# Where the next block's planes are cast and subtracted at the seams of a split-precision MLP

## The chip, the core and the metric

The kernel runs on one core of a Trainium2 chip. The core has five engines, each with its own queue of instructions that it works off in order: TensorE (PE, matmuls; its weight loads are shown as PEld), VectorE (DVE), ScalarE (ACT), GpSimd (POOL) and SyncE (SP, which here only issues DMAs). Engines wait for each other on semaphores. The metric is the device time of one execution in microseconds; the figure for the kernel before is the median of three runs.

## The reference

A transformer block with adaptive layer norm on one sequence of S = 2048 rows of D = 448, all float32: six modulation rows from `c`, attention with 16 heads, then an MLP with F = 1792.

```python
x = A_x
mod = (_silu(c) @ w_mod).reshape(c.shape[0], 6, 1, -1)
sa, ca, ga, sb, cb, gb = (mod[:, 0], mod[:, 1], mod[:, 2], mod[:, 3], mod[:, 4], mod[:, 5])
h = _layernorm(x, axis=-1) * (1 + ca) + sa
x = x + ga * _A_ref(h, A_wqkv, A_wo)
h = _layernorm(x, axis=-1) * (1 + cb) + sb
x = x + gb * _B_ref(h, B_w1, B_b1, B_w2, B_b2)

def _B_ref(x, w1, b1, w2, b2):
    y = _layernorm(x, axis=-1)
    h = _gelu(jnp.einsum("bsd,df->bsf", y, w1) + b1)
    return jnp.einsum("bsf,fd->bsd", h, w2) + b2
```

The change lies in `_B_ref`, the MLP, alone.

## The kernel before, in words

**Stages.** The kernel first makes the modulation rows, q, k and v, then runs attention (most of the span), and ends with the MLP, which takes the stretch from about 820 us on. The instructions are issued in an order written out by hand: each engine's queue holds its instructions in the order in which the Python code emits them.

**Split precision.** A float32 operand of a matmul is cut into two planes of the matmul's type: "hi", a rounded copy, and "lo", what is left when hi is subtracted. A product is then hi·hi + hi·lo + lo·hi, so making an operand ready costs one cast and one subtraction, and the subtraction needs the cast.

**The MLP.** The rows are worked in NB = 4 blocks b of 512 rows, the hidden features in NFT = 14 tiles i of 128. For every (b, i), `mlp1` (L1418) runs a W1 chain of eleven matmuls (L396), applies the gelu on ScalarE (L1428), casts its result (L1431, on ScalarE for block 0 and on VectorE for the others) and subtracts on VectorE (L1432). `mlp2` (L1456) multiplies the two planes of a gelu by W2, twelve matmuls of lines 1472 to 1474, and after the fourteenth tile adds and stores the block (L1478, L1479). The loop at L1482 issues `mlp1` of step n and `mlp2` of step n - LAG, LAG = 2, so a gelu has about two chains and two W2 blocks of time until TensorE wants it. The W1 chains take their accumulators in turn from a ring of three.

**The order inside a W1 chain** is that of `terms448` (L400): for each of the planes k = 0, 1, 2 of the block's rows, hi times both planes of W1 (six matmuls), then the three lo planes (three), then plane 3, which holds both its hi rows and its lo rows (two).

**The next block's rows.** `ln2_stages` (L1105 onwards) gives two functions for each block. `stage(i)` holds the second layer norms, spread over the steps of the block before; for blocks 1 to 3 it ends with a transpose on VectorE, a store to a scratch tensor in DRAM (`send`, L1142) and a load of four chunks in turned order (`fetch`, L1152). For block 1 the fetch is issued at step i = 11 of block 0, for blocks 2 and 3 at step i = 9 of the block before. `chunk(k)` (L1177), for k = 0 to 3, makes the planes: the cast `act.copy` on ScalarE (L1192) and the subtraction on VectorE (L1193). Block 0 takes the transposes on TensorE in place of the fetch; it isn't reached by the change.

**Room for the planes.** A block has seven plane tiles: hi of k = 0 to 2, lo of k = 0 to 2, and the shared one of k = 3. They take their places from eight tags in a ring (L1180), so plane n of a block takes the place that plane n - 1 of the block before had, and plane 0 takes the spare one.

**A seam** is the step of (b, 13) with b = 0, 1 or 2, the last of a block. Before the change it issues, in this order: the W1 chain of (b, 13), its gelu, cast and subtraction; W1 and W2 tiles that are still to be prepared (`w_prep.step()`, L1490, only in block 0: at its last step a product with the row gb on VectorE at L1240, a cast on ScalarE at L1242 and a subtraction on VectorE at L1243); chunks 0 and 1 of the next block; `mlp2(b, 11)`; chunks 2 and 3. Then follow the chain of (b + 1, 0) and `mlp2(b, 12)`.

```python
yT[b] = (lambda k: tiles[k] if k < 3 else tiles[6], lambda k: tiles[3 + k])
...
act.copy(hi, p)
dve.tensor_tensor(out=lo[rs_], in0=p[rs_], in1=f(hi)[rs_], op=ALU.subtract)
```

Of the kernel before, what the change touches and what calls it, by code (L numbers as in the profile page):

```python
# [26 lines left out]
NC = 4  # L27
NB = S // 512
NG = H // 4
NKT = S // 128  # L30
NFT = F // 128
# [13 lines left out]
def tile_adaln_block(ctx: ExitStack, tc: tile.TileContext, x, wqkv, wo, w1, b1, w2, b2, c, w_mod, out):  # L45
# [29 lines left out]
    def nm(t):  # L75
        uid[0] += 1
        return f"{t}_{uid[0]}"

    def sbt(tag, shape, dt=F32, bufs=1):
        return sb.tile(shape, dt, tag=tag, name=nm(tag), bufs=bufs)  # L80
# [27 lines left out]
    def ps_mx():  # L108
        mx_ring.append(mx_ring.pop(0))
        return ps_tile(mx_ring[-1], 1 if mx_ring[-1] == "m1" else 2)  # L110
# [7 lines left out]
    def f(t):  # L118
        return t.bitcast(F32)
# [272 lines left out]
    def mm_acc(p, terms, mid=None):  # L392
        for i, (a, b) in enumerate(terms):
            if mid and i == len(terms) // 2:
                mid()
            pe.matmul(p, a, b, start=(i == 0), stop=(i == len(terms) - 1))  # L396
# [3 lines left out]
    def terms448(x_hi, x_lo, w_hi, w_lo):  # L400
        ts = []
        for k in range(3):
            ts += [(x_hi(k), w_hi(k)), (x_hi(k), w_lo(k))]
        ts += [(x_lo(k), w_hi(k)) for k in range(3)]
        ts += [(x_hi(3), w_lo(3)), (x_hi(3), w_hi(3))]
        return ts
# [411 lines left out]
    for b in range(NB):  # L818
# [12 lines left out]
        for n, (tb, kind, g) in enumerate(tasks):  # L831
# [9 lines left out]
            k = n - (6, 4, 4, 4)[b]  # L841
# [19 lines left out]
            if more:  # L861
                k = n - (6, 4, 4, 4)[b]
# [417 lines left out]
    lnst = [ln2_stages(b) for b in range(NB)]  # L1280
# [134 lines left out]

    ov = out[0].rearrange("(b p t) n -> b p t n", p=128, t=4)

    def mlp1(b, i):  # L1418
        q, ii = divmod(i, 4)
        w_hi, w_lo = w1t[q]  # L1420
        fs = slice(ii * 128, (ii + 1) * 128)
        p = ps_mx()
        ts = terms448(*yT[b], lambda k: w_hi(k)[:, fs], lambda k: w_lo(k)[:, fs])
        mm_acc(p, [(w, y) for y, w in ts])
        gf = sbt("full", [128, 512], bufs=3)
        if (b, i) == (0, 0):
            act.activation(gf[:, 0:1], zero_col, AF.Gelu_apprx_tanh)
        act.activation(gf, p, AF.Gelu_apprx_tanh, bias=b1_col[:, i : i + 1])  # L1428
        ghi = sbt("hi", [128, 512], F32R, bufs=3)
        glo = sbt("lo", [128, 512], F32R, bufs=3)  # L1430
        (dve.tensor_copy if b else act.copy)(ghi, gf)  # L1431
        dve.tensor_tensor(out=glo, in0=gf, in1=f(ghi), op=ALU.subtract)  # L1432
        gs[(b, i)] = (ghi, glo)

    load_o(NB - 2, 2, "c1")
    load_o(NB - 2, 3, "c0h")
    mlp1(0, 0)
    av(*pend)
    end_unit(pend[0], pend[3])
# [16 lines left out]
    def mlp2(b, m):  # L1456

        if m == 0 and b < NB - 1:
            om[b] = [s2[:, j] for s2 in (ps_s2(), ps_s2()) for j in range(2)]
        elif m == 0:  # L1460
            for key in ("s1", "s0"):
                ps_close(key)
            for t in range(4):
                ps_open(f"t{t}")
            om[b] = [ps_tile(f"t{t}") for t in range(4)]
        ghi, glo = gs.pop((b, m))
        q, ii = divmod(m, 4)
        w_hi, w_lo = w2t[q][0](ii), w2t[q][1](ii)
        for t in range(4):
            ts = slice(t * 128, (t + 1) * 128)  # L1470
            pp = om[b][t][:, :D]
            pe.matmul(pp, ghi[:, ts], w_hi, start=(m == 0), stop=False)  # L1472
            pe.matmul(pp, ghi[:, ts], w_lo, start=False, stop=False)  # L1473
            pe.matmul(pp, glo[:, ts], w_hi, start=False, stop=(m == NFT - 1))  # L1474
        if m == NFT - 1:
            for t in range(4):
                ot = xn_t()
                dve.tensor_tensor(out=ot[:, :D], in0=om[b][t][:, :D], in1=acc[b][:, t, :], op=ALU.add)  # L1478
                sp.dma_start(ov[b][:, t, :], ot[:, :D])  # L1479

    seq = [(b, i) for b in range(NB) for i in range(NFT)]
    for n in range(len(seq) + LAG):  # L1482
        if n < len(seq):
            b, i = seq[n]
            if n:
                mlp1(b, i)
            for fn in tail.pop(n, ()):
                fn()
            for _ in range(2 if n % 2 else 1):
                w_prep.step()  # L1490
            if b + 1 < NB:
                lnst[b + 1][0](i)
            if b:
                lnst[b][0](20 + i)
        ahead = n < len(seq) and i == NFT - 1 and b + 1 < NB
        if ahead:
            for k in range(2):
                lnst[b + 1][1](k)
        if n >= LAG:
            mlp2(*seq[n - LAG])  # L1500
        if ahead:
            for k in range(2, NC):
                lnst[b + 1][1](k)
    for key in ("t3", "t2", "t1", "t0", "m2", "m1", "o"):
        ps_close(key)

# [34 lines left out]
```

## Time and profile before

| | |
|---|---|
| median of three runs | 1099.84 us (1099.55 to 1100.01) |
| the profiled execution's own time | 1099.75 us |
| its span in the profile | 1097.5 us |
| granted TensorE clock | 1.00 |
| W1 chain, eleven matmuls | 2.56 us |
| a gelu on ScalarE (L1428) | 0.69 us |
| a cast of a plane (L1192), alone | 0.62 us |
| a subtraction of a plane (L1193), alone | 0.68 us |

How to read it: the profile is of one execution, times are from the start of its span, and the time of a run is 2.25 us longer than the span. In a timeline row stand the start, the duration, the engine, the line of the kernel, the operation, what it writes and reads, the count of instructions that were merged, and in brackets the idle time ahead of it on its engine with what ended it. Consecutive instructions of one engine overlap a little, so a merged row of four is shorter than four single ones. In a list of waits a row names who waited, for whom, the sum in us, the number of times and the longest.

### The profile page before, as it was taken

What the parts mean: (1) busy time and instruction counts of PE and PEld (TensorE: products, weight loads), DVE (VectorE), ACT (ScalarE), POOL (GpSimd) and SP (SyncE); (2) the same over time, 40 slices, a digit from 0 to 9 for tenths busy, and PEclk for the clock granted to TensorE, in tenths of its full rate; (3) what the DMA queues carried; (4) which work ended last, traced back from release to release, by engine and by line L of the source; (5) the groups of instructions that cost most, each with busy time, mean ns of one, the idle gap of its engine ahead of it and who ended that gap; (6) DMA issues with size and microseconds to landing.
All of it is one profiled execution on the core that took longest, in us unless ns stands there. A gap on an engine that the chain in (4) does not pass through costs nothing.

```text
span 1097.5 us, 20709 instructions
## 1 busy us (share of the span) xinstructions
PE 1088.1 (99%) x8255; PEld 658.3 (60%) x8255; DVE 805.1 (73%) x1382; ACT 697.6 (64%) x883; POOL 198.7 (18%) x201
## 2 busy tenths in 40 slices
PE   8999999999999999999999999999999999999998
PEld 6756675444444444444444444554488788888887
DVE  6968788999999999988888888575655565463322
ACT  4565667888888888888888888678933411211211
POOL 1543332210000000000000000217123042061000
PEclk9999999999999999999999999999999999999999
DMA  9563354121222201232211213111442302002000
GB/s 312 207 190 103 97 188 134 59 65 32 72 76 64 77 28 41 67 98 54 69 48 38 86 49 104 58 31 59 136 137 65 101 34 55 18 34 72 34 1 34
DMA packets 58438, 88.57 MB, mean 81 GB/s; under 512 B 13759, under 2 KB 25686, under 8 KB 58330
## 3 DMA queue, kind: packets, MB, share of 16 engines
q1 hardware_dynamic: 57858, 86.51, 26.3%
q8 instruction: 65, 1.06, 0.4%
q10 hardware_dynamic: 148, 0.46, 0.1%
q0 software_dynamic: 336, 0.28, 0.1%
q14 instruction: 31, 0.25, 0.1%
HBM read 59.39 MB, written 29.50 MB: 81 GB/s over the span
## 4 chain that ended last, share of the span: by engine, by line
PE 96%; DVE 2%; DMA 1%; ACT 1%; issue 0%; SPq 0%; DVEq 0%; ACTq 0%
PE s L1382 23%; PE o L1337 23%; PE m L396 16%; PE pa L396 9%; PE m L476 8%; PE s L1472 3%; PE s L1473 3%; PE s L1474 3%; PE s L476 2%; PE t L1473 1%; PE t L1474 1%; PE t L1472 1%; DVE y L1193 1%; DMA slot_c<-in_w_mod_dram 1%; PE o L277 1%; DVE mxp L481 0%
## 5 line engine op out<-in xcount | busy, mean ns | idle before, releaser
L481 DVE TENSOR_REDUCE mxp<-m 128x1 f32<-128x512 f32 x555 | 359.7, 685 | 65.0 <-PE m L476 49.6
L1382 PE MATMUL s<-slot_b,slot_a 28*128 28x512 f32 (+1 forms) x3072 | 356.7, 423 | 0.0
L1382 PEld LDWEIGHTS s<-slot_b,slot_a 28*128 28x128 f32 (+1 forms) x3072 | 211.1, 183 | 176.0 <-ACT slot_c L1395 96.4
L476 PE MATMUL m<-kh,qh 28*128 28x512 f32 x607 | 226.9, 468 | 0.5 <-DVE mxp L481 0.3
L1395 ACT ACTIVATE slot_c<-s 128x1024 f32<-128x1024 f32 x170 | 174.7, 1028 | 51.6 <-PE s L1382 50.8
L1337 PE MATMUL o<-slot_c,v 128*32 128x512 f32 x680 | 178.9, 605 | 0.0
L1428 ACT ACTIVATE full<-m,b_col 128x512 f32<-128x512 f32 x56 | 38.6, 689 | 206.6 <-PE m L396 201.4
L686 DVE TENSOR_REDUCE mxp<-s 128x2 f32<-128x1024 f32 x107 | 131.1, 1226 | 5.1
L1337 PE MATMUL o<-slot_c1h,v 128*32 128x512 f32 x512 | 134.7, 605 | 0.0
L1337 PE MATMUL o<-slot_c0h,v 128*32 128x512 f32 x508 | 133.6, 605 | 0.0
L1395 ACT ACTIVATE slot_c1h<-s 128x1024 f32<-128x1024 f32 x128 | 130.7, 1021 | 0.0
L1395 ACT ACTIVATE slot_c0h<-s 128x1024 f32<-128x1024 f32 x127 | 130.5, 1028 | 0.0
L1395 ACT ACTIVATE slot_d<-s 128x1024 f32<-128x1024 f32 x86 | 88.4, 1028 | 25.0 <-PE s L1382 24.7
L1431 DVE CAST hi<-full 128x512 fp32r<-128x512 f32 x42 | 18.7, 444 | 112.3 <-ACT full L1428 112.3
L476 PEld LDWEIGHTS m<-kh,qh 28*128 28x128 f32 x607 | 90.7, 182 | 15.2 <-DVE mxp L481 13.1
L1337 PE MATMUL o<-slot_d,v 128*32 128x512 f32 x344 | 90.5, 605 | 0.4 <-ACT osb L1301 0.4
L1062 POOL TENSOR_TENSOR osb<-osb,osb 128x512 f32<-128x512 f32 x16 | 20.6, 1286 | 362.8 <-DMA osb<-drec 343.5
L1432 DVE TENSOR_TENSOR lo<-full,hi 128x512 fp32r<-128x512 f32 x56 | 46.0, 822 | 29.7 <-ACT hi L1431 25.1
L396 PE MATMUL m<-y,slot_a 128*128 128x512 f32 x160 | 60.9, 397 | 0.4 <-DVE y L1193 0.2
L481 DVE TENSOR_REDUCE mxp<-ma 128x1 f32<-128x512 f32 x61 | 39.5, 681 | 13.2 <-PE m L476 9.2
L1337 PEld LDWEIGHTS o<-slot_c,v 128*32 128x32 f32 x680 | 24.5, 108 | 39.1 <-issue 36.5
L650 DVE CUSTOM_DVE_ANT_0 slot_d0i<-m,slot_d0i 128x512 f32<-128x512 f32 x54 | 37.3, 691 | 14.3 <-PE m L476 11.3
(351 smaller groups left out, 1824.2 us busy)
## 6 DMA issues: line engine op xcount, KB each, us to landing
slot_b<-d SPq DMA_DIRECT2D x32, 256.0 KB
slot_a<-d SPq DMA_DIRECT2D x32, 256.0 KB
d<-lo SPq DMA_DIRECT2D x28, 256.0 KB
d<-hi SPq DMA_DIRECT2D x16, 256.0 KB
osb<-drec SPq DMA_DIRECT2D x15, 256.0 KB
out_dram<-xn SPq DMA_DIRECT2D x16, 224.0 KB
raw<-in_B_w_dram SPq DMA_DIRECT2D x14, 224.0 KB
qh<-d SPq DMA_DIRECT2D x12, 256.0 KB
```

The source lines that it names most:

```text
L396: pe.matmul(p, a, b, start=(i == 0), stop=(i == len(terms) - 1))
L476: pe.matmul(m, qh_sb[(g, qt)][js, i * 128 : (i + 1) * 128], k[js, :], start=True, stop=True)
L481: dve.tensor_reduce(out=mxp[(g, qt)][:, i, j, cch : cch + 1], in_=m, op=ALU.max, axis=AX.X)
L686: dve.tensor_reduce(out=mxp[(g, qt)][:, i, j : j + 2, cch], in_=t, op=ALU.max, axis=AX.X)
L1337: pe.matmul(o[32 * j : 32 * j + 32, :], v_sb[kt // 4][:, kt % 4, 4 * g + j, :], p[j // 2][:, j % 2, :], start=(kt == 0), stop=(kt == NKT - 1),
L1382: pe.matmul(s2[:, jj, :], ks[rows_, kp, kc], qs[rows_, qp, :], start=(term == 0), stop=(term == 2))
L1395: act.activation(pt[hf], s2, AF.Exp, scale=SCALE)
L1428: act.activation(gf, p, AF.Gelu_apprx_tanh, bias=b1_col[:, i : i + 1])
L1432: dve.tensor_tensor(out=glo, in0=gf, in1=f(ghi), op=ALU.subtract)
L1472: pe.matmul(pp, ghi[:, ts], w_hi, start=(m == 0), stop=False)
L1473: pe.matmul(pp, ghi[:, ts], w_lo, start=False, stop=False)
L1474: pe.matmul(pp, glo[:, ts], w_hi, start=False, stop=(m == NFT - 1))
```

## The change

The four calls of `chunk` for the next block move from behind the step's other work into `mlp1`, between the last matmul of the chain of (b, 13) and the gelu that reads it. `mlp1` gets an argument `mid`, a function that is called there; `seam(b)` gives one that calls the four chunks of block b. It is passed at i = 13 of blocks 0, 1 and 2 only.

```diff
-    def mlp1(b, i):
+    def mlp1(b, i, mid=None):
         q, ii = divmod(i, 4)
...
         mm_acc(p, [(w, y) for y, w in ts])
+        if mid:
+            mid()
         gf = sbt("full", [128, 512], bufs=3)
...
+    def seam(b):
+        return lambda: [lnst[b][1](k) for k in range(NC)]
+
     seq = [(b, i) for b in range(NB) for i in range(NFT)]
     for n in range(len(seq) + LAG):
         if n < len(seq):
             b, i = seq[n]
             if n:
-                mlp1(b, i)
+                mlp1(b, i, seam(b + 1) if i == NFT - 1 and b + 1 < NB else None)
...
-        ahead = n < len(seq) and i == NFT - 1 and b + 1 < NB
-        if ahead:
-            for k in range(2):
-                lnst[b + 1][1](k)
         if n >= LAG:
             mlp2(*seq[n - LAG])
-        if ahead:
-            for k in range(2, NC):
-                lnst[b + 1][1](k)
```

## The prediction

> **What bounds the kernel now.** I read the page's head first, then the list of waits from 820 us on (the MLP's stretch), then the timeline around each of the three places where one block of 512 rows gives way to the next.
>
> ```profile
> span 1097.5 us, 20709 instructions
> PE 1088.1 (99%) x8255; PEld 658.3 (60%) x8255; DVE 805.1 (73%) x1382; ACT 697.6 (64%) x883; POOL 198.7 (18%) x201
> ```
>
> TensorE is busy 1088.1 of 1097.5 us, so an edit that removes no matmul can win only what TensorE stands idle. Who makes it wait in the MLP:
>
> ```profile
> PE m L396 <- ACT y L1192: 1.4, 1, 1.4
> PE m L396 <- DVE y L1193: 0.2, 1, 0.2
> PEld m L396 <- ACT y L1192: 2.2, 3, 1.7
> PEld m L396 <- DVE y L1193: 1.6, 3, 0.5
> ```
>
> All four rows are W1 matmuls (line 396) that wait for the next block's planes: L1192 is the cast, L1193 the subtraction. The PE and PEld rows show the same idle time twice, so the rows are not added up; the timeline gives the sum. First seam (block 0 to 1), TensorE:
>
> ```profile
> 875.21 0.37 PE L1474 MATMUL s<-slot_d0i,lo 128*128 128x448 f32 x1
> 876.94 0.50 PE L396 MATMUL m<-y,slot_b 128*128 128x512 f32 x1 [1.36 <-ACT y L1192]
> 879.60 0.50 PE L396 MATMUL m<-y,slot_a 128*128 128x512 f32 x1 [0.19 <-DVE y L1193]
> 880.17 0.37 PE L1472 MATMUL s<-slot_e,hi 128*128 128x448 f32 x1
> 882.38 0.36 PE L1474 MATMUL s<-slot_e,lo 128*128 128x448 f32 x1
> 885.13 0.37 PE L1472 MATMUL s<-slot_e,hi 128*128 128x448 f32 x1
> ```
>
> From the last W2 matmul ahead of a W1 chain to the first one behind it are 885.13 - 882.38 = 2.75 us where nothing is late (second chain of block 1) and 880.17 - 875.21 = 4.96 us at the seam. **Lost: 2.21 us.** Seams two and three:
>
> ```profile
> 947.59 0.37 PE L1474 MATMUL s<-slot_d0i,lo 128*128 128x448 f32 x1
> 950.13 0.19 PEld L396 LDWEIGHTS m<-y,slot_a 128*128 128x128 f32 x1 [0.52 <-DVE y L1193]
> 950.70 0.37 PE L1472 MATMUL s<-slot_e,hi 128*128 128x448 f32 x1
> 952.97 0.37 PE L1474 MATMUL s<-slot_e,lo 128*128 128x448 f32 x1
> 955.73 0.37 PE L1472 MATMUL s<-slot_e,hi 128*128 128x448 f32 x1
> 1018.21 0.37 PE L1474 MATMUL s<-slot_d0i,lo 128*128 128x448 f32 x1
> 1020.74 0.19 PEld L396 LDWEIGHTS m<-y,slot_a 128*128 128x128 f32 x1 [0.51 <-DVE y L1193]
> 1021.32 0.37 PE L1472 MATMUL s<-slot_e,hi 128*128 128x448 f32 x1
> ```
>
> Here the interval is 3.11 us twice, against 955.73 - 952.97 = 2.76: **0.35 us each**, and only the last subtraction is late. All three seams lose 2.21 + 0.35 + 0.35 = 2.91 us. The bound on any gain is therefore about 2.9 us.
>
> Why the planes are late at the first seam, on ScalarE and then VectorE:
>
> ```profile
> 870.85 0.57 ACT L1242 CAST slot_e<-full 128x448 fp32r<-128x448 f32 x1 [1.34 <-DVE full L1240]
> 873.17 0.69 ACT L1428 ACTIVATE full<-m,b_col 128x512 f32<-128x512 f32 x1 [1.75 <-PE m L396]
> 873.89 0.62 ACT L1431 CAST hi<-full 128x512 fp32r<-128x512 f32 x1
> 875.80 0.56 ACT L1242 CAST slot_e<-full 128x448 fp32r<-128x448 f32 x1 [1.29 <-DVE full L1240]
> 876.27 2.18 ACT L1192 CAST y<-xn 128x512 fp32r<-128x512 f32 x4
> ...
> 874.54 0.69 DVE L1432 TENSOR_TENSOR lo<-full,hi 128x512 fp32r<-128x512 f32 x1 [2.47 <-ACT hi L1431]
> 875.15 0.62 DVE L1240 TENSOR_TENSOR full<-raw,row_gb 128x448 f32<-128x448 f32 x1
> 876.40 0.63 DVE L1243 TENSOR_TENSOR slot_e<-full,slot_e 128x448 fp32r<-128x448 f32 x1 [0.63 <-ACT slot_e L1242]
> 876.94 2.61 DVE L1193 TENSOR_TENSOR y<-xn,y 128x512 fp32r<-128x512 f32 x4
> ```
>
> The four casts stand on ScalarE behind a ladder: gelu, its copy, VectorE's subtraction, VectorE's product with the row gb, then the cast of the last W2 tile at 875.80. That cast is the releaser, not the data: ScalarE goes straight from it to the plane casts. At seams two and three there is no W2 tile; the casts come right behind the gelu, and the subtractions behind the gelu's own cast and subtraction:
>
> ```profile
> 945.60 0.69 ACT L1428 ACTIVATE full<-m,b_col 128x512 f32<-128x512 f32 x1 [4.32 <-PE m L396]
> 946.19 2.17 ACT L1192 CAST y<-xn 128x512 fp32r<-128x512 f32 x4
> ...
> 946.86 0.69 DVE L1432 TENSOR_TENSOR lo<-full,hi 128x512 fp32r<-128x512 f32 x1
> 947.47 2.61 DVE L1193 TENSOR_TENSOR y<-xn,y 128x512 fp32r<-128x512 f32 x4
> ```
>
> **The change part by part.** It adds and removes no instruction: 12 casts and 12 subtractions move. For blocks 1 to 3 chunk() issues only those two, no matmul and no DMA, so the queues of TensorE, SP and POOL stay as they are. Splitting the calls two and two around mlp2 changes no queue either, since mlp2(b, 11) issues matmuls alone. What changes is the order on two engines: on ScalarE the four casts stand ahead of gelu(b, 13), on VectorE the four subtractions ahead of that gelu's subtraction (and its cast at seams two and three), and at seam one ahead of the W2 tile.
>
> What the casts now wait for. (a) Room: through the ring of eight tags, plane n of the new block takes the place of plane n-1 of the old one; the first plane takes the spare tag. So the casts and subtractions release one by one as the chain of (b, 13) reads its planes, the last after its ninth matmul of eleven. A chain's pace:
>
> ```profile
> 882.74 2.56 PE m L396 x11
> ```
>
> 0.233 us a matmul, so the last room comes 2 x 0.233 = 0.47 us before the chain's end. Were the whole chain the releaser (upper bound), all casts but the first would begin at its end. (b) Data: at seams two and three the fetch was issued some 16 us earlier. At seam one it is close:
>
> ```profile
> 869.08 2.42 SPq L1152 DMA_DIRECT2D xn<-y_dr  x5
> 874.00:874.50 0.50, 0.50 (x4) 0.47 (x3) 0.00 (x0) 0.50 (x1) 0.00 (x0) 1.00 0.28 82
> 874.50:875.00 0.50, 0.50 (x4) 0.46 (x3) 0.46 (x1) 0.01 (x1) 0.00 (x0) 1.00 0.00 0
> ...
> 929.50:930.00 0.50, 0.50 (x4) 0.41 (x3) 0.00 (x0) 0.00 (x0) 0.00 (x0) 1.00 0.00 0
> 929.84 0.34 SPq L1152 DMA_DIRECT2D xn<-y_dr  x1
> ```
>
> In these rows of stretches the last two numbers are the DMA engines' busy share and GB/s. The five fetches of the first seam are out of SP by 871.5 and the DMA engines fall silent at 874.5. How long the signal follows the last byte isn't shown for these transfers; at the second seam the fetch that waits for the stores goes out at 929.84, with traffic gone by 929.5, so about 0.3 us. Latest arrival of all four chunks then: 874.8. Earliest for the first, if they land in order (four parts of about 1.2 us between 869.6 and 874.4): near 871.
>
> Seam one, new order, with arrivals at 871.0, 872.2, 873.4, 874.8. A cast takes 2.18 / 4 = 0.54 us, a subtraction 2.61 / 4 = 0.65. Casts are done by about 872.0, 872.8, 874.0, 875.4, subtractions by 872.7, 873.5, 874.7, 876.1. TensorE needs the first plane at 875.41 (one step of 0.2 us after 875.21), the first subtraction six matmuls later at 876.8, the last at 877.5. Nothing is late: **2.2 us recovered**. With all four arriving at 874.8, the casts end at 875.4, 875.9, 876.4, 877.0 and the subtractions at 876.1, 876.7, 877.4, 878.0: the last is 0.5 us late, so 1.7 us recovered. I take the full 2.2, being nearest the row of the SP queue, where the requests went out one after another.
>
> Seams two and three: the casts are over within 0.2 us of the chain's end (945.6), or at 945.6 + 3 x 0.54 = 947.2 under the upper bound of (a), the last subtraction by 947.1 or 948.6. TensorE wants it at 947.8 + 9 x 0.233 = 949.9. **0.35 us each**, by both bounds.
>
> What is pushed back. gelu(b, 13) starts up to 1.6 us later at seams two and three (upper bound of (a)), 2.2 to 3.8 us later at seam one (875.4 to 877.0 in place of 873.17). Behind it wait its high and low parts, needed by mlp2(b, 13), which stands two chains and two W2 blocks on: at seam one 875.41 + 2.56 + 2.41 + 2.56 = 882.9. From the gelu's start to the end of its low part are 874.54 + 0.69 - 873.17 = 2.06 us, so 877.5 to 879.1: at least 3.8 us spare. Behind it on VectorE comes the last W2 tile, needed at the same 882.9: from the low part on 0.62 + 0.63 + 0.56 = 1.8 us, so 880.9 at the latest, 2 us spare. The accumulator that gelu(b, 13) frees is wanted three chains later. So the push costs nothing, covered by those two chains; without that cover it would cost its 2.2 to 3.8 us.
>
> After the seam everything is paced by TensorE and moves up with it; no load is outstanding that could come due sooner. Sum: 1099.75 us (profiled execution; 1097.5 span plus 2.25 around it) - 2.9 = 1096.85. The median, 1099.84, stands 0.09 higher, hence **1096.9 us**.
>
> [...]
>
> **The rivals.** *The fetch is the real releaser at seam one.* For: it is the one seam with the big loss, and the DMA engines were busy until 874.5. Against: the W2 tile's cast ends exactly where the plane casts begin, and its 1.29 us of idle time are put down to VectorE. The rows allow arrival no later than 876.3 for the first chunk. Then the first cast starts where it does now, the subtractions behind it end where they do now, and seam one gives nothing; with the 0.7 of the others the time is 1099.1, and less for arrivals between 874.8 and 876.3. Chance 0.11.
>
> *The new order does nothing*, because the queues are not what the text says or the waits for room make up for what was won: 1099.8. Against: at 945.60 to 946.19 the first cast starts with mlp2 still running, so room doesn't hang on later work. Chance 0.05.
>
> *Slower: ScalarE is parked on the fetch.* The casts now stand ahead of the gelu, so a late chunk would hold gelu(0, 13), its parts and the W2 tile, in order. It decides once the first cast can't start before about 877: with arrival at 879.0 the last subtraction ends near 881.9, the chain at 882.6 instead of 880.17, 2.4 lost and 0.7 won: 1101.5. Against: the old cast ran at 876.27 with nothing missing, and the fetch's own queue is not touched. Chance 0.04.
>
> **How the numbers follow.** Forecast 0.80, with 1096.6 to 1097.6 as its own range (gain 2.9, or 2.4 with late arrivals, and 0.23 for half the spread of the three runs). Fetch 0.11, nothing 0.05, slower 0.04. The range for 8 in 10 runs from 1096.4 to 1098.6; it leaves out the last two cases and the upper half of the fetch case. A measurement of this kernel tells about 0.2% from no change, 2.2 us: faster is below 1097.6. The forecast lies 0.7 us clear of that, so nearly all of it counts: faster 0.79, same 0.17, slower 0.04.
>
> **What would show it.** In the new profile the rows of L1192 and L1193 as releasers of L396 should be gone from the list of waits; at the first seam the W1 chain should follow the last W2 matmul by about 0.2 us, and the interval of 4.96 us should read about 2.75, the two of 3.11 about 2.76. The plane casts should start ahead of the gelu near 871.5 to 874.8, and the gelu near 875.5. The total of TensorE's busy time should hardly move. I am wrong if ScalarE idles before L1192 past 875.4 with the fetch as releaser, if mlp2(0, 13) waits for L1432 or L1243, or if the seams close and the time comes back elsewhere, as at the store of a finished block (L1478).

## The result and the profile after

The changed kernel takes 1097.72 us (median of 14 runs, 1096.78 to 1098.61); the kernel before, run beside it, 1100.15 us (14 runs). The ratio is 0.9976 with a 95% interval of 0.9969 to 0.9984: 2.6 us faster, between 1.8 and 3.4. The span of the profiled execution went from 1097.5 to 1094.6 us, 2.9 less. In the changed kernel's code the lines behind `mlp1` have moved by two: the gelu is L1430, its cast and subtraction L1433 and L1434, the W2 matmuls L1474 to L1476, the store's additions L1480.

The head of the page after, which shows that TensorE does the same work in a shorter span:

```profile
span 1094.6 us, 20712 instructions
PE 1087.0 (99%) x8255; PEld 658.8 (60%) x8255; DVE 805.7 (74%) x1382; ACT 697.8 (64%) x883; POOL 198.8 (18%) x201
```

The list of waits after, from 820 us on. The rows in which L396 waited for L1192 or L1193 are gone. The planes' own instructions now wait instead, for the chain that frees their room and, at the first seam, for the fetch; TensorE's weight loads wait only at the store of a block:

```profile
ACT y L1192 <- PE m L396: 4.3, 4, 1.7
DVE y L1193 <- PE m L396: 3.8, 2, 1.9
ACT y L1192 <- DMA xn<-y_dr: 1.5, 2, 0.9
PEld s L1474 <- DVE xn L1480: 0.9, 2, 0.6
```

The timeline after around the first seam, TensorE first, then ScalarE and VectorE:

```profile
875.10 0.37 PE L1476 MATMUL s<-slot_d0i,lo 128*128 128x448 f32 x1
875.31 0.39 PE L396 MATMUL m<-y,slot_b 128*128 128x512 f32 x1
877.86 0.37 PE L1474 MATMUL s<-slot_e,hi 128*128 128x448 f32 x1
882.84 0.37 PE L1474 MATMUL s<-slot_e,hi 128*128 128x448 f32 x1
...
872.18 1.39 ACT L1192 CAST y<-xn 128x512 fp32r<-128x512 f32 x2 [0.92 <-DMA xn<-y_dr]
874.16 1.28 ACT L1192 CAST y<-xn 128x512 fp32r<-128x512 f32 x2 [0.59 <-DMA xn<-y_dr]
875.35 0.68 ACT L1430 ACTIVATE full<-m,b_col 128x512 f32<-128x512 f32 x1
877.98 0.57 ACT L1242 CAST slot_e<-full 128x448 fp32r<-128x448 f32 x1 [1.29 <-DVE full L1240]
...
874.82 1.41 DVE L1193 TENSOR_TENSOR y<-xn,y 128x512 fp32r<-128x512 f32 x2 [0.52 <-ACT y L1192]
878.58 0.62 DVE L1243 TENSOR_TENSOR slot_e<-full,slot_e 128x448 fp32r<-128x448 f32 x1 [0.63 <-ACT slot_e L1242]
```

The first W1 matmul follows the last W2 matmul by 0.21 us, as anywhere else, and the interval over the chain is 877.86 - 875.10 = 2.76 us; it was 4.96. The casts are paced by the arriving chunks (two idle gaps with the fetch as releaser), the gelu starts at 875.35 instead of 873.17, and the last W2 tile is ready at 878.58 + 0.62 = 879.2. The W2 block that wants both begins at 882.84 and waits for neither.

At the second seam it is the room that paces the casts, one plane after the other while the chain of (1, 13) still runs:

```profile
941.45 1.15 ACT L1192 CAST y<-xn 128x512 fp32r<-128x512 f32 x2 [1.67 <-PE m L396]
943.08 0.62 ACT L1192 CAST y<-xn 128x512 fp32r<-128x512 f32 x1 [0.48 <-PE m L396]
943.60 0.68 ACT L1430 ACTIVATE full<-m,b_col 128x512 f32<-128x512 f32 x1
...
945.58 0.37 PE L1476 MATMUL s<-slot_d0i,lo 128*128 128x448 f32 x1
948.34 0.37 PE L1474 MATMUL s<-slot_e,hi 128*128 128x448 f32 x1
```

The interval is 2.76 us, against 3.11 before; the third seam reads the same. The W2 block behind the chain of (1, 13) begins at 943.34 and the gelu starts at 943.60, no later behind its chain than a gelu elsewhere, so here nothing is pushed back at all.

One wait has grown, at the store of block 0. The W2 block of (1, 0) waits there for the additions on VectorE:

```profile
888.12 0.19 PEld L1474 LDWEIGHTS s<-slot_v,hi 128*128 128x128 f32 x1 [0.57 <-DVE xn L1480]
886.92 2.21 DVE L1480 TENSOR_TENSOR xn<-s,acc 128x448 f32<-128x448 f32 x4
```

The same weight load had waited 0.29 us before the change, so about 0.3 us is given back here. From the first W2 matmul of (0, 11) to the very last matmul the MLP took 1093.57 - 872.97 = 220.60 us before and 1090.70 - 872.86 = 217.84 after: 2.76 us less. That is 2.91 from the seams, less the 0.3 given back, plus about 0.15 won in small steps in the blocks right behind the second and the third seam. This stretch is used below, since it leaves out what attention varies by (the stretch begins at 872.97 us before and at 872.86 after).

### The profile page after: what moved, and what is told of

The parts are those of the page before. It is cut to its first block, busy times and chain, and to the rows that moved or that the text cites. A ratio compares the mean times of both kernels' runs of the same rounds, so it can differ in the third digit from the quotient of the medians.

```text
span 1094.6 us, 20712 instructions
## 1 busy us (share of the span) xinstructions
PE 1087.0 (99%) x8255; PEld 658.8 (60%) x8255; DVE 805.7 (74%) x1382; ACT 697.8 (64%) x883; POOL 198.8 (18%) x201
## 4 chain that ended last, share of the span: by engine, by line
PE 97%; DVE 1%; DMA 1%; ACT 0%; issue 0%; SPq 0%; ACTq 0%; DVEq 0%
PE s L1382 23%; PE o L1337 23%; PE m L396 17%; PE pa L396 9%; PE m L476 8%; PE s L1474 3%; PE s L1475 3%; PE s L1476 3%; PE s L476 2%; PE t L1475 1%; PE t L1476 1%; PE t L1474 1%; DMA slot_c<-in_w_mod_dram 1%; PE o L277 1%; DVE mxp L481 0%; PE ma L476 0%
## 5 line engine op out<-in xcount | busy, mean ns | idle before, releaser
L1430 ACT ACTIVATE full<-m,b_col 128x512 f32<-128x512 f32 x56 | 38.6, 689 | 197.3 <-PE m L396 197.3
L1433 DVE CAST hi<-full 128x512 fp32r<-128x512 f32 x42 | 18.7, 445 | 106.0 <-ACT full L1430 105.9
L1434 DVE TENSOR_TENSOR lo<-full,hi 128x512 fp32r<-128x512 f32 x56 | 46.0, 822 | 27.3 <-ACT hi L1433 22.9
L396 PE MATMUL m<-y,slot_a 128*128 128x512 f32 x160 | 60.7, 395 | 0.0
```

## The experiments

All times are ratios to the kernel before, run on the same chip, with their 95% intervals. "Intervals" are those of the three seams, from the last W2 matmul ahead of the chain to the first behind it.

**One seam at a time.** The first two kernels apply the new order to part of the seams and keep the old calls around `mlp2` at the rest.

```diff
-                mlp1(b, i, seam(b + 1) if i == NFT - 1 and b + 1 < NB else None)
+                mlp1(b, i, seam(b + 1) if i == NFT - 1 and b == 0 else None)
...
```

> The new order at the first seam alone (block 0 to 1); the other two seams keep the old order. Theory (the planes are late because of what stands ahead of them on ScalarE and VectorE, seam by seam): the interval from the last W2 matmul ahead of the chain to the first one behind it is 2.76 us at the first seam and stays 3.11 us at the other two; 2.2 us less than before, ratio 0.9980. Rival (a common shift, or seconds won elsewhere): the intervals of seams two and three move too, or the time falls by clearly more or less than the first seam's interval.

Measured: 0.9983 (0.9974 to 0.9992), intervals 2.76, 3.10 and 3.11 us, stretch 218.69 us. The first seam alone brings 1.9 us in the stretch: its 2.2 less the longer wait at the store, which is there at 0.6 us too.

```diff
-                mlp1(b, i, seam(b + 1) if i == NFT - 1 and b + 1 < NB else None)
+                mlp1(b, i, seam(b + 1) if i == NFT - 1 and 0 < b < NB - 1 else None)
...
```

> The new order at the second and third seam alone. Theory: the first seam's interval stays 4.96 us, the other two read 2.76 us; 0.7 us less than before, ratio 0.9994, too small to be told from 1 by the times, so the intervals decide. Rival (the two small waits only move to another place): TensorE shows a new wait of 0.3 us behind each seam, and the span is that of before.

Measured: 0.9992 (0.9982 to 1.0001), not to be told from 1; intervals 4.97, 2.76 and 2.76 us, stretch 219.76 us, 0.84 less than before. No new wait of TensorE shows behind the seams. The two parts, 1.91 and 0.84, add up to 2.75, against 2.76 for the whole: the seams are independent.

**What of the old queue was in the way.** The third kernel issues the chunks behind the gelu and its subtraction, but ahead of the last W2 tile's preparation.

```diff
-                mlp1(b, i, seam(b + 1) if i == NFT - 1 and b + 1 < NB else None)
+                mlp1(b, i)
+                if i == NFT - 1 and b + 1 < NB:
+                    seam(b + 1)()
```

> The four chunks are issued behind gelu, copy and subtraction of (b, 13), but ahead of the preparation of the last W2 tile. Theory (at the first seam the ladder through the W2 tile makes nearly all of the wait, the gelu only the 0.35 us that it costs at the other seams too): casts begin near 874.4 us, first-seam interval about 3.1 us, the others stay 3.11; 1.85 us less than before, ratio 0.9983. Rival (it is the place ahead of the gelu that counts): the first-seam interval stays above 4 us. Rival (arrival of the fetched chunks counts): ScalarE idles before the casts with the fetch as releaser and the interval lies between.

Measured: 0.9988 (0.9978 to 0.9997), intervals 3.17, 3.09 and 3.10 us, stretch 218.61 us, 2.0 less than before. This is the timeline of its ScalarE at the first seam:

```profile
874.18 0.69 ACT L1430 ACTIVATE full<-m,b_col 128x512 f32<-128x512 f32 x1 [1.80 <-PE m L396]
874.91 0.62 ACT L1433 CAST hi<-full 128x512 fp32r<-128x512 f32 x1
875.43 2.18 ACT L1192 CAST y<-xn 128x512 fp32r<-128x512 f32 x4
```

Four casts without a gap right behind the gelu's copy: neither the gelu nor the fetch made the big wait. Of the first seam's 2.2 us, 1.8 were the W2 tile's ladder and 0.4 the gelu with its parts, the 0.35 of the other seams.

The fourth kernel keeps the old order and only moves all four chunks behind `mlp2(b, 11)`.

```diff
-        if ahead:
-            for k in range(2):
-                lnst[b + 1][1](k)
         if n >= LAG:
             mlp2(*seq[n - LAG])
         if ahead:
-            for k in range(2, NC):
+            for k in range(NC):
```

> The old place, but all four chunks behind the W2 block of (b, 11) and none ahead of it. Theory (that block issues matmuls alone, so no queue changes): intervals 4.96, 3.11 and 3.11 us, ratio 1.0000. Rival (the split around the W2 block was part of the wait): the first-seam interval grows by up to the W2 block's 2.4 us.

Measured: 1.0002 (0.9992 to 1.0012), intervals 4.97, 3.11 and 3.12 us, stretch 220.60 us. The place around the W2 block is worth nothing, as it holds no work of ScalarE or VectorE.

**How much the fetch has in hand.** The next two move transpose, store and fetch of block 1 by one step of block 0, in the new and in the old order.

```diff
-                plan.setdefault(10 if b < 2 else 7 + t // 2, []).append(lambda t=t: turn(t))
+                plan.setdefault(11 if b < 2 else 7 + t // 2, []).append(lambda t=t: turn(t))
...
-            plan.setdefault(10 if b < 2 else 8, []).append(send)
-            plan.setdefault(11 if b < 2 else 9, []).append(fetch)
+            plan.setdefault(11 if b < 2 else 8, []).append(send)
+            plan.setdefault(12 if b < 2 else 9, []).append(fetch)
```

> The new order, with transpose, store and fetch of block 1 one step later (steps 11 and 12 of block 0 in place of 10 and 11), so that its chunks arrive about 5 us later, the first near 877.1 us. Theory (the gain at the first seam holds only as long as the chunks are there in time; a parked ScalarE costs nothing beyond the wait for the planes, as two chains and two W2 blocks cover the gelu behind it): TensorE waits for the planes, first-seam interval about 6.6 us, no wait of the W2 block of (0, 13) for its gelu's planes or its W2 tile; about 1.0 us slower than the kernel before. Rival (parking costs extra): that W2 block waits for L1434 or L1243, and the time is 3 us or more above the kernel before.

> The old order with the same later fetch. Theory: the fetch now sets the first seam in either order, interval about 6.6 us, the other seams 3.11; about 1.7 us slower than the kernel before, that is 0.7 us slower than the new order with the late fetch. Rival (the old order hides a late fetch better, since it has other work for ScalarE meanwhile): a first-seam interval at least 1 us shorter than in the new order with the late fetch.

Measured: 1.0023 (1.0011 to 1.0035) and 1.0028 (1.0017 to 1.0039); first-seam intervals 8.01 and 8.02 us. The two orders are indeed alike once the fetch is late, and in neither does a W2 block wait for a gelu's planes or for the W2 tile, so a parked ScalarE costs nothing of its own. But both seams lost 1.4 us more than the 6.6 expected, and the times are off by as much. The new order with the late fetch shows why. Here are three rows of its timeline at the first seam, then its stretches (length, then TensorE, PEld, VectorE, ScalarE and GpSimd busy, then the granted clock, DMA share and GB/s):

```profile
878.01 0.50 PE L396 MATMUL m<-y,slot_b 128*128 128x512 f32 x1 [2.39 <-ACT y L1192]
880.11 0.80 PE L396 MATMUL m<-y,slot_b 128*128 128x512 f32 x1 [0.71 <-ACT y L1192]
880.09 1.41 DVE L1193 TENSOR_TENSOR y<-xn,y 128x512 fp32r<-128x512 f32 x2 [0.75 <-ACT y L1192]
...
875.00:878.00 3.00, 0.62 (x4) 0.22 (x2) 0.01 (x1) 0.63 (x2) 0.00 (x0) 1.00 0.91 272
878.00:880.00 2.00, 1.39 (x4) 0.59 (x4) 1.33 (x2) 1.17 (x2) 0.00 (x0) 0.81 0.37 116
880.00:882.00 2.00, 1.89 (x5) 1.50 (x6) 1.41 (x3) 1.88 (x4) 0.00 (x0) 0.50 0.00 0
882.00:884.00 2.00, 2.00 (x6) 1.64 (x5) 1.37 (x3) 0.77 (x2) 0.00 (x0) 0.50 0.00 0
884.00:886.00 2.00, 2.00 (x7) 1.77 (x6) 1.90 (x4) 0.38 (x1) 0.00 (x0) 0.50 0.00 0
886.00:888.00 2.00, 2.00 (x11) 1.75 (x10) 1.05 (x4) 0.00 (x0) 0.00 (x0) 0.98 0.00 0
```

Behind the wait the granted clock was 0.50 for nearly 7 us, and the matmuls there ran slowly too (those of the W1 chain 0.43 us apart rather than 0.233). The last subtraction ended at 880.09 + 1.41 = 881.50; an estimate with the two matmuls behind it at 0.233 us gives an interval of about 6.7 us, so about 1.3 of the 8.01 are the clock. The runs agree: each kernel has one execution whose mean granted clock stayed at 1.00, and these took 1101.52 and 1101.95 us, 1.2 and 1.7 above the kernel before, where 1.0 and 1.7 were expected. The gap of 0.7 us between the orders could not be read from the medians, as the halved clock lasted longer in some executions than in others (the mean granted clock runs from 0.996 to 1.00 over the two kernels' executions, and in the profiled ones the W2 block behind the seam took 3.72 us in the new order and 2.40 in the old).

The opposite move, one step sooner in the old order, asks whether the fetch ever held the old casts.

```diff
-                plan.setdefault(10 if b < 2 else 7 + t // 2, []).append(lambda t=t: turn(t))
+                plan.setdefault(9 if b < 2 else 7 + t // 2, []).append(lambda t=t: turn(t))
...
-            plan.setdefault(10 if b < 2 else 8, []).append(send)
-            plan.setdefault(11 if b < 2 else 9, []).append(fetch)
+            plan.setdefault(9 if b < 2 else 8, []).append(send)
+            plan.setdefault(10 if b < 2 else 9, []).append(fetch)
```

> The old order, with transpose, store and fetch of block 1 one step sooner (steps 9 and 10 of block 0), so that its chunks are there about 5 us sooner. Theory (in the old order the planes wait for their turn on ScalarE, not for the fetched data): casts still begin right behind the W2 tile's cast, first-seam interval stays 4.96 us, time that of the kernel before. Rival (the fetch is the real releaser): the casts begin sooner and the interval shrinks towards 2.76 us.

Measured: 1.0037 (1.0022 to 1.0051), 4 us slower where no change was expected; but the first-seam interval stays 4.97 us. Its SP queue ahead of that seam, ScalarE at the seam, and two rows of its list of waits:

```profile
865.73 1.16 SPq L1211 DMA_DIRECT2D raw<-in_B_w_dram  x1
869.00 2.43 SPq L1152 DMA_DIRECT2D xn<-y_dr  x5
...
880.67 0.56 ACT L1242 CAST slot_e<-full 128x448 fp32r<-128x448 f32 x1 [1.29 <-DVE full L1240]
881.14 2.18 ACT L1192 CAST y<-xn 128x512 fp32r<-128x512 f32 x4
...
PEld m L396 <- DVE slot_c1h L1222: 2.5, 1, 2.5
PEld m L396 <- ACT y L1192: 2.2, 3, 1.7
```

The chunks were asked for 12.1 us ahead of the casts, where it was 876.27 - 869.08 = 7.2 before, and the casts still began right behind the W2 tile. So the old order was bound by its queue, not by data. (The lead comes from the seam's being later: the fetch goes out at nearly the same time as before.) The 4 us come from elsewhere: on the SP queue the store of block 1 now stands ahead of the load of the last W1 piece (L1211), which goes out at 865.73 and not at 857.32. A W1 chain had to wait for its plane (L1222), which lengthened that chain's interval by 2.4 us, and with half the clock for about 3.4 us behind it the next W2 block took 1.5 us longer.

**The cover of what is pushed back.** LAG = 1 lets a W2 block follow its gelu one chain sooner, in both orders.

```diff
-    LAG = 2
+    LAG = 1
```

> The new order with LAG = 1: the W2 block of (b, 13) follows one chain sooner, so the cover of what is pushed back is 5 us shorter. Theory: first-seam interval 2.76 us, but the W2 block of (0, 13) now stands right behind it and waits for the last W2 tile, whose planes end near 878.5 and 879.2 us against 877.9: 1.1 to 1.3 us lost there, so the first seam keeps about 1.0 of its 2.2 us. Rival (the push costs nothing in any case): no wait there, and the time is 2.9 us below the old order with LAG = 1.

> The old order with LAG = 1, to set beside the new order with LAG = 1. Theory: seams as in the kernel before (4.96, 3.11, 3.11 us), no wait of the W2 block of (0, 13), time within 1 us of the kernel before. Rival: a shorter lag costs by itself, with new waits of W2 blocks for L1432.

Measured: 0.9982 (0.9971 to 0.9993) and 0.9997 (0.9985 to 1.0008). The old order has its seams at 5.00, 3.14 and 3.15 us and no other wait. In the new order no chain waits, but the W2 block of (0, 13) does:

```profile
883.30 0.47 PE L1474 MATMUL s<-slot_e,hi 128*128 128x448 f32 x1 [0.59 <-ACT slot_e L1242]
883.96 0.48 PE L1475 MATMUL s<-slot_e,hi 128*128 128x448 f32 x1 [0.18 <-DVE slot_e L1243]
```

The last W2 matmul ahead of this chain starts at 879.78, so without a wait the block would begin 2.76 us later, at 882.54. The first matmul comes 883.30 - 882.54 = 0.76 us late and the second, with 0.20 us for a W2 matmul, another 0.46: 1.2 us. From the last W2 matmul ahead of the first seam to the very last matmul the two kernels take 1093.65 - 879.78 = 213.87 and 1093.43 - 877.84 = 215.59 us. The difference of 1.7 us is what 2.9 less 1.2 leaves, and the ratios, 0.0015 apart, agree with it. The push is free only under the cover of the second chain.

**What is left.** The last variant issues the final W2 block of a block of rows, with its four additions, ahead of the next layer norm's statistics.

```diff
+            store = n >= LAG and seq[n - LAG][1] == NFT - 1
+            if store:
+                mlp2(*seq[n - LAG])
             if b + 1 < NB:
                 lnst[b + 1][0](i)
             if b:
                 lnst[b][0](20 + i)
-        if n >= LAG:
+        if n >= len(seq) or (n >= LAG and not store):
             mlp2(*seq[n - LAG])
```

> The new order, and the last W2 block of a block of rows with its four additions (L1480) is issued ahead of the layer-norm step of the same step of the loop, so the additions stand on VectorE ahead of the statistics of the block after next. Theory (the 0.57 and 0.28 us for which the first W2 weights of a new block wait for L1480 come from those statistics, about 1.6 us on VectorE, standing ahead): both waits vanish, the time falls by a further 0.4 us or so against the new order, ratio to the kernel before 0.9974, which the times alone cannot tell from 0.9976. Rival (the additions wait for the matmuls, not for VectorE): the two waits stay.

Measured: 0.9971 (0.9958 to 0.9983). Both waits for L1480 are gone, and no wait of TensorE is left in the MLP's list; stretch 217.31 us. It was run again beside the changed kernel on one chip.

> The changed kernel as it is, on the same chip as the variant that issues the store first. Theory: no TensorE wait for planes, the MLP from the W2 block of (0, 11) to the last matmul 217.8 us long, 2.8 us shorter than before (220.6); ratio 0.9975. Rival (some of the gain was luck of one execution): a stretch above 218.5 us.

> The variant with the store's additions ahead of the statistics, on the same chip as the changed kernel. Theory: the same stretch 217.3 us, 0.5 us shorter than the changed kernel's; ratio 0.9970, the two ratios' intervals overlapping. Rival (the statistics that come later delay the next block's planes or normalisation): a wait of TensorE that the changed kernel doesn't have.

Measured: changed kernel 0.9974 (0.9964 to 0.9984), 1097.35 us, stretch 217.85 us; store first 0.9971 (0.9961 to 0.9982), 1097.15 us, stretch 217.31 us. By the stretch the variant is 0.54 us ahead, twice alike; by the times the two cannot be told apart. It is the best version found. From the W2 block of (0, 11) on, its TensorE shows as busy throughout (217.58 of 217.58 us), so the profile has no wait left there that another order could win.

## Why the prediction was right

**The sum.** The 2.91 us lost at the seams were to be won whole, and they were: intervals of 4.96, 3.11 and 3.11 us became 2.76, 2.76 and 2.75. The forecast of 1096.9 us stands 0.8 below the median of 1097.72, which is in the range given for 8 in 10 runs but 0.1 above the narrower one of the forecast itself. Of the 0.8, 0.3 is the kernel before, which read 1100.15 in the larger set of runs and not 1099.84; the rest is the gain, 2.4 by the medians and 2.6 by the ratio against 2.9, with 2.9 inside the ratio's interval. The 0.3 given back at the store is part of it.

**The bound.** As a bound on any gain 2.9 us was too low. The list of waits before has one more row of TensorE in the MLP, at the store of a block:

```profile
PEld s L1472 <- DVE xn L1478: 0.5, 2, 0.3
```

With the store's additions issued first the stretch was 220.60 - 217.31 = 3.29 us shorter than before. The step from TensorE's busy time to the bound was also loose: in this stretch the time in which TensorE does not show as busy went from 220.93 - 219.19 = 1.74 us to 218.14 - 218.01 = 0.13, only 1.6 us less where 2.76 were won. Matmuls that overlap (0.37 us long, 0.20 apart) count the end of the last one ahead of a wait as busy; the intervals from start to start, on which the sum rests, don't.

**Queue, not data, at the first seam.** Right: with the data asked for sooner the old interval didn't move, and with the W2 tile alone out of the way 1.8 of the 2.2 us were won.

**Arrival of the chunks.** ScalarE's idle gaps, which the fetch ends, last until 872.18 and 874.16, so the 871.0 and 873.4 assumed for the first and third chunk were 1.2 and 0.8 us early. It did no harm: the last subtraction ended at 874.82 + 1.41 = 876.23, and the matmul that reads it, nine steps of 0.233 us behind 875.31, starts at 877.4. The gelu's start was put at 875.4 and came at 875.35. That is partly luck, as the last cast stood without a gap behind the late third one, so that the gelu's start doesn't show when the fourth chunk came. For the step from the last byte to the cast the trace gives a bound: traffic ended by about 874.1, with a share of 0.03 in the half microsecond behind 874.0, and the last cast began by 874.82, so at most about 0.7 us lies between.

**Room.** The ring of tags frees one plane at a time, as argued, and at the later seams the gelu isn't pushed at all; the upper bound of 1.6 us wasn't needed.

**What is pushed back costs nothing.** Right for this kernel, and its condition was measured: without the second chain the W2 tile is late by 1.2 us. With both chains the tile was ready at 879.2, where 880.9 was put as the latest.

**The rivals.** The fetch as releaser, no effect, and the parked ScalarE fell. The price of parking, 2.4 us at the first seam for an arrival at 879.0, left the clock out: with the late fetch the seam lost 8.01 - 4.96 = 3.05 us, of which about 1.3 are the halved clock by the estimate above. In the working of that rival the last subtraction would end, by its own rates of 0.54 and 2.61 us, near 882.15 and not at 881.9; the chain's end at 882.6 fits the later figure. And with a late fetch the wait falls on both orders alike, so it would have been no cost of the new order.

**"The time comes back elsewhere, as at the store of a finished block (L1478)."** It did, in small: about 0.3 us at the store of block 0. The gelu of (1, 1) started 0.54 us behind the start of the W2 block that follows its chain, instead of 0.26, and the work on VectorE ahead of the additions came as much later. What delays that gelu stays open; the wait itself vanishes with the store's additions issued first.

## What to carry to other kernels

Where an engine that isn't the bound makes the bound one wait, look at what stands directly ahead of the late instruction on its own queue: an idle gap put down to some other engine can be a ladder that the late work has no part in (here 1.8 of the first seam's 2.2 us). Moving the urgent work ahead was free while what it displaces had slack and cost 1.2 us with one chain less of it, so count that slack to its reader in chains, and check that the urgent work's data is there, since the queue behind it now waits for that data too (with the late fetch the gelu's subtraction, L1434, began at 881.97 and not at 876.72). The stretch of the stage concerned told two versions 0.54 us apart here, where the ratios of whole runs, 0.9974 (0.9964 to 0.9984) and 0.9971 (0.9961 to 0.9982), could not.

## What the runs showed of the hardware

A wait of TensorE cost more than its length in three of the profiled executions, by about 1.3 us in the new order with the late fetch, by the estimate above. In the kernel before, 1.36 us of idle time at the first seam left the granted clock at 1.00. In the profiled execution of the new order with the late fetch, gaps of 2.39 and 0.71 us with four matmuls between them were followed by a granted clock of 0.50 for about 6.8 us; in the old order with the late fetch 2.07 and 1.05 us by about 3.4 us of it; and with the W1 piece late, one gap of 2.11 us by about 3.4 us. It doesn't follow in every execution: each kernel with the late fetch has one whose mean granted clock is 1.00, though only the profiled ones show their gaps. At 0.50 the matmuls of a W2 block ran 0.37 us apart rather than 0.20.
